# A fused attention and gated-MLP block: first pair of the last stage reordered, one store moved behind the last drain, another to a different queue

## The chip, the cores and the metric

The kernel runs on one core of one Trainium2 chip. The core has four computing engines that each work through a queue of their own in order: TensorE (PE), VectorE (DVE), ScalarE (ACT) and GpSimd (POOL). SyncE (SP) only issues transfers, and POOL issues some too. Sixteen DMA engines move the bytes. The metric is the device time of one execution in microseconds, as a median over several.

## The reference

All of it works on a normalised input `xn` of 2048 rows by 512 columns, in fp32:

```
xn  = layernorm(x)
q, k, v = split(xn @ wqkv)                    # 32 heads of 16
phi(t) = [softmax(t @ w_phi), softmax(-t @ w_phi)]    # per head, 32 features
kv  = phi(k)^T v ;  z = sum over rows of phi(k)
A   = (phi(q) kv) / (phi(q) z + 1e-6) @ wo
zz  = gelu(xn @ w_in) ;  z1, z2 = halves of zz (688 columns each)
g   = w_sp @ layernorm(z2) + b_sp             # w_sp: 2048 x 2048
B   = (z1 * g) @ w_out
out = x + A + B
```

## The kernel before

The 2048 rows are 16 tiles of 128. fp32 products are built from three matmuls: each operand is split into a rounded part and the rest (`round_h` on ACT, `rest_l` on DVE), and `mm3` (lines 52 to 55) multiplies high by high, high by low and low by high.

There are three stages. The first projects q, k, v and the MLP's first half, and writes the exponentials of q to HBM (`e_d`). The second multiplies `w_sp` by the normalised `z2`, with a seven-product scheme for 2 x 2 blocks, in eight rounds of two row tiles; `products` issues the matmuls, `drain` adds the seven PSUM tiles up, `gate` multiplies by z1, transposes the result on DVE (L732) and gives back a function that stores it block by block to HBM (`u_d`, four DMAs of 128-byte runs). The seventh round's gate (i = 6, `NP - 2`) is called inside the loop; the eighth round's drain stands behind the loop, and its gate is called late in the third stage, after the pair of tiles 8 and 9.

The third stage, which the change touches, handles the 16 query tiles in pairs. For a pair it

- finishes the features of each tile (`q_fin`, L487 to L494, eight DVE operations on a tile `et` loaded from `e_d`; tiles 0 and 1 come ready made as `eq`). From tile 4 on POOL copies the finished tile to a tile `er` by DMA (L842);
- transposes them on PE (`attend_T`: `ptq`, copied to `f` by ACT);
- multiplies by the key-value matrix `kvT` (`attend`: `po`, split into `oT` by ACT and DVE);
- multiplies the gated rows `u` (loaded by SP as `u` and `rt`, split into `uh` and `ul` by `gated`) by w_out into a PSUM tile `pout` (`project_u`);
- adds `oT` times wo to the same `pout` (`project_o`), adds the tile of x (`xr`, loaded by SP) on DVE (L913), and SP stores the sum to `out`.

There are two `pout` banks, so `project_u` of the next pair needs the xr addition of this one. `wof` are the raw rows of wo on their way to `wo_h` and `wo_l`.

The order on each engine is not written out: a scheduler places the instructions by its own estimate of when each is ready, in the order of the program text otherwise, and `tc.issue_after(x)` keeps what is inside it from being placed before x. Tiles of a pool that has been closed give their memory to later tiles, and a later tile waits for the last user of each byte it takes. A wait stands in the queue of the engine that issues, so everything behind it in that queue waits too. In the program before, the first pair is written out ahead of the loop (`project_u` 0, transposes, `project_u` 1, attention product), and the other pairs are in the loop.

Of the kernel before, what the change touches and what calls it, by code (L numbers as in the profile page):

```python
# [18 lines left out]
P = 128  # L19
# [18 lines left out]
def mixer(ctx: ExitStack, tc: tile.TileContext, x, x_t, wv, wqkT, phi_bd, wo, w_in, wst, b_r, w_out, out):  # L38
# [4 lines left out]
    def round_h(eng, h, src):  # L43
        if eng is act:
            return act.activation(h, src, AF.Copy).ins  # L45
        return eng.tensor_copy(h, src).ins

    def rest_l(l, src, h, eng=None):
        return (eng or dve).tensor_tensor(l, src, h.bitcast(F32), op=ALU.subtract).ins  # L49
# [429 lines left out]
    def load_q(s, et):  # L479
        sp.dma_start(et[:, :NF + 2 * H], e_d[s])  # L480
        return et

    def q_fin(et, tmp, zb):

        e, r, t, w = et[:, :NF], *(et[:, NF + k * 2 * H:NF + (k + 1) * 2 * H] for k in range(3))
        den = et[:, NF + 6 * H:QW]
        dve.tensor_tensor(tmp, e, zb, op=ALU.mult)  # L487
        dve.tensor_reduce(t, heads(tmp), axis=AX.X, op=ALU.add)
# [5 lines left out]
        return e, dve.tensor_tensor(heads(e), heads(e), bc(w, 2 * H), op=ALU.mult).ins  # L494
# [227 lines left out]
    def gate(i, cb, z, u, ut, after=None):  # L722
        cb, first, _ = cb
        with tc.issue_after(after or first):
            act.activation(z[:, :, :FH], z[:, :, :FH], AF.Gelu_apprx_tanh)
        zs = z[:, :, :FH].rearrange("p k (j f) -> p k j f", j=2)
        us = u[:, :, :FH].rearrange("p k (j f) -> p k j f", j=2)
        dve.tensor_tensor(us, zs, cb, op=ALU.mult)
        lo, hi = u[:, :, KF * P:FH], u[:, :, FH:FU].bitcast(F32R)
        dve.tensor_copy(hi, lo)  # L730
        rest_l(lo, lo, hi)
        dve.transpose(ut.rearrange("p k f -> p (k f)"), u.rearrange("p k f -> p (k f)"))  # L732

        def store():
            src = ut.rearrange("p k f -> p (k f)")
            dst = u_d[2 * i:2 * i + 2].rearrange("k (j a) t -> a (k j) t", a=BL)
            for b in range(0, P, BL):
                (sp if i < NP - 2 else pool).dma_start(dst[:, :, b:b + BL], src[b:b + BL].rearrange("p (m b) -> p m b", b=BL))

        return store  # L740

    def slot(name, dt=F32):
        return xz.tile([P, 2, FH], dt, tag="xz", name=name).rearrange("p a b -> p (a b)")
# [27 lines left out]
    lasts, wu = [None] * 7, []  # L771

    def first_q(s):
        e = slot("eq", F32R)[:, :NF]
        sp.dma_start(e.bitcast(F32), e_d[s, :, :NF])
        return e
# [12 lines left out]
    for n in range(NC):  # L789
        i = SEQ[n][0]  # L790
        if n % NQ == 1 and i < NP - 1:
            z = load_z1(i)
        products(n, g)
        if n % NQ == NQ - 1 and i < NP - 1:
            c = gt.tile([P, 2, FU], F32, tag="c", name="c")
            cq = c[:, :, :FH].rearrange("p k (j f) -> p k j f", j=2)
            cb = drain(i, g, cq)
            g = {}
        if n + 3 < NC:
            raw[n + 3] = load_a(n + 3)  # L800
        if n + 2 < NC:
            A[n + 2] = prep_a(n + 2, raw.pop(n + 2))
        if n % NQ == NQ - 1 and i < NP - 1:
            gate(i, cb, z, c, z, prep_a.last)()
        if n == NC - 4:
            stage_w()
        if n == NC - 3:
            zs = slot("zb", F32R)
            zb, ident_r = zs[:, :NF].bitcast(F32), zs[:, NF:NF + P]
            round_h(act, ident_r, ident)  # L810
            sp.dma_start(zb, zb_d)
            uT = [first_gate(0)]
            es[0], es[1] = first_q(0), first_q(1)
        if n == NC - 2:
            t = slot("u1", F32R)
            us = {1: load_u(1, k_tiles(t[:, :KF * P]).bitcast(F32), t[:2 * REM, KF * P:(KF + 1) * P])}
            ets[2], ets[3] = (load_q(s, slot("et")) for s in (2, 3))
    cb = drain(NP - 1, g, slot("c").rearrange("p (k j f) -> p k j f", k=2, j=2))
    with tc.issue_after(cb[1]), tc.issue_after(cb[2]):
        es[2], last = q_fin(ets.pop(2), slot("qtmp")[:, :NF], zb)  # L820
    mid.close()


# [32 lines left out]
    def attend_T(s):  # L856

# [15 lines left out]
    def attend(fs):  # L873

        oT = [wk.tile([P, NG, 2 * P], F32R, tag=f"oT{k}", name="oT") for k in "hl"]
        po = [pso.tile([P, 2, 2 * P], F32, tag="po", bufs=2, name="po") for _ in range(2)]
        for m in range(H // 2):
            k, c, r = m // 8, m // 2 % 4, m % 2  # L880
            rows, cols = slice(r * HP, (r + 1) * HP), slice(r * QP, (r + 1) * QP)
            lasts[3] = pe.matmul(po[r][c * QP:(c + 1) * QP, k], kvT[rows, m // 2, cols], fs[m // 4][rows, m // 2 % 2],
                                 start=True, stop=True).ins
        for r in range(2):
            qs = slice(r, None, 2)
            round_h(act, oT[0][:, qs], po[r])
            ins = rest_l(oT[1][:, qs], po[r], oT[0][:, qs])
        return oT, ins
# [26 lines left out]

    GATE_LAST = 8

    wo_h, wo_l = (cw.tile([P, ND, D], F32R, name=f"wo{k}") for k in "hl")
# [12 lines left out]
    def ahead(i):  # L931

        if 3 < i + 3 < NT:
# [2 lines left out]
            ets[i + 4] = load_q(i + 4, slot("et"))  # L936
            us[i + 4] = fetch_u(i + 4)

    nxt = {}
    for i in range(0, NT, 2):  # L940
        if i:
            p[i] = project_u(i, nxt.pop(i))
            if i + 2 < NT:
                nxt[i + 2] = gated(us.pop(i + 2))
            with tc.issue_after(lasts[2]):
                oT, _ = attend(fT)
            with tc.issue_after(lasts[3]):
                p[i + 1] = project_u(i + 1, nxt.pop(i + 1))
        else:
            nxt[2] = gated(us.pop(2))  # L950
        if i + 3 < NT:
            nxt[i + 3] = gated(us.pop(i + 3))
        for k in range(2):
            project_o(i + k, oT, p.pop(i + k))
            ahead(i + k)
        if i == 2:
            with tc.issue_after(lasts[6]):
                z = load_z1(NP - 1)
        if i == GATE_LAST:
            with tc.issue_after(lasts[0]), tc.issue_after(lasts[1]):  # L960
                gate(NP - 1, cb, z, z, gt.tile([P, 2, FU], F32, tag="zt", name="zt"))()
            p2.close()
        if i + 2 < NT:
            with tc.issue_after(lasts[4]):
                fT = attend_T(i + 2)
# [33 lines left out]
```

## Time and profile before

| | |
|---|---|
| median of 3 runs | 634.07 us (632.37 to 634.67) |
| the profiled execution | 633.23 us |
| its span | 631.5 us |
| granted TensorE clock | 1.00 |
| PE busy in the span | 621.9 us (98%) |
| DVE busy in the span | 517.8 us (82%) |
| last matmul of the second stage to the end | 495.2 to 631.5 us |

Times in a timeline are microseconds from the start of the span. A row of a timeline gives start, duration, engine, source line, operation and tiles; in brackets stands how long the engine was idle before it and what ended that. A duration is that of one instruction, and DVE and PE overlap the end of one with the start of the next, so the spacing of starts is what a chain of them costs. A row of a DMA view gives the issues, the size and the time from issue to landing. Line numbers are those of the kernel before; from line 732 on those of the changed kernel are 2 to 6 higher.

### The profile page before, as it was taken

What the parts mean: (1) busy time and instruction counts of PE and PEld (TensorE: products, weight loads), DVE (VectorE), ACT (ScalarE), POOL (GpSimd) and SP (SyncE); (2) the same over time, 40 slices, a digit from 0 to 9 for tenths busy, and PEclk for the clock granted to TensorE, in tenths of its full rate; (3) what the DMA queues carried; (4) which work ended last, traced back from release to release, by engine and by line L of the source; (5) the groups of instructions that cost most, each with busy time, mean ns of one, the idle gap of its engine ahead of it and who ended that gap; (6) DMA issues with size and microseconds to landing.
All of it is one profiled execution on the core that took longest, in us unless ns stands there. A gap on an engine that the chain in (4) does not pass through costs nothing.

```text
span 631.5 us, 11445 instructions
## 1 busy us (share of the span) xinstructions
PE 621.9 (98%) x4406; PEld 564.9 (89%) x4406; DVE 517.8 (82%) x908; ACT 270.9 (43%) x431; POOL 93.7 (15%) x176
## 2 busy tenths in 40 slices
PE   8999999999999999999999999999999989999997
PEld 6888888888888999999999999999999868877776
DVE  5999998987987768889989688696978789989622
ACT  5643434443333638877444343253444322223220
POOL 4142121111011015332000000000002001101100
PEclk9999999999999999999999999999999999999999
DMA  8455465354336941002463745637467798886930
GB/s 315 163 102 143 114 162 152 87 139 134 106 94 170 300 170 67 1 2 68 146 132 119 180 90 157 145 100 176 89 189 244 234 286 286 302 294 203 217 119 33
DMA packets 83574, 98.40 MB, mean 156 GB/s; under 512 B 40672, under 2 KB 53728, under 8 KB 83520
## 3 DMA queue, kind: packets, MB, share of 16 engines
q1 hardware_dynamic: 73088, 61.30, 33.1%
q0 software_dynamic: 8128, 30.74, 17.6%
q10 hardware_dynamic: 2304, 5.64, 2.3%
q8 instruction: 34, 0.56, 0.4%
q14 instruction: 20, 0.16, 0.1%
HBM read 56.37 MB, written 26.61 MB: 131 GB/s over the span
## 4 chain that ended last, share of the span: by engine, by line
PE 93%; DMA 2%; DVE 2%; SPq 1%; issue 0%; ACT 0%; POOL 0%; DVEq 0%; ACTq 0%; POOLq 0%
PE g L55 11%; PE g L54 11%; PE g L53 11%; PE proj L55 7%; PE proj L53 7%; PE proj L54 7%; PE zps L55 6%; PE zps L53 6%; PE zps L54 6%; PE pout L53 4%; PE pout L55 4%; PE pout L54 4%; DMA er<-et 2%; PE ptq L867 1%; PE kvps L312 1%; SPq L748 1%
## 5 line engine op out<-in xcount | busy, mean ns | idle before, releaser
L54 PE MATMUL g<-B,A 128*128 128x344 f32 x448 | 143.2, 320 | 0.0
L53 PE MATMUL g<-B,A 128*128 128x344 f32 x448 | 143.1, 319 | 0.0
L55 PE MATMUL g<-B,A 128*128 128x344 f32 x448 | 142.9, 320 | 0.0
L53 PEld LDWEIGHTS g<-B,A 128*128 128x128 f32 x448 | 84.2, 188 | 0.0
L55 PEld LDWEIGHTS g<-B,A 128*128 128x128 f32 x448 | 84.1, 188 | 0.0
L54 PEld LDWEIGHTS g<-B,A 128*128 128x128 f32 x448 | 84.1, 188 | 0.0
L45 ACT ACTIVATE A<-S 128x512 fp32r<-128x512 f32 x64 | 39.3, 628 | 77.5 <-DVE S L532 56.0
L113 ACT ACTIVATE e<-e,r_x 128x1024 f32<-128x1024 f32 x28 | 32.2, 1150 | 47.1 <-DVE e L112 46.6
L53 PE MATMUL proj<-wqk_h,xT 128*128 128x512 f32 x128 | 50.9, 398 | 0.0
L55 PE MATMUL proj<-wqk_h,xT 128*128 128x512 f32 x128 | 50.6, 395 | 0.0
L54 PE MATMUL proj<-wqk_l,xT 128*128 128x512 f32 x128 | 50.3, 393 | 0.0
L49 DVE TENSOR_TENSOR A<-S,A 128x512 fp32r<-128x512 f32 x64 | 43.3, 687 | 6.8 <-ACT A L45 6.6
L45 ACT ACTIVATE A<-wf 128x512 fp32r<-128x512 f32 x64 | 33.3, 521 | 31.7 <-PE g L55 14.9
L53 PE MATMUL zps<-w_0h,xT 128*128 128x344 f32 x128 | 41.4, 323 | 0.0
L55 PE MATMUL zps<-w_0h,xT 128*128 128x344 f32 x128 | 41.1, 321 | 0.0
L53 PE MATMUL zps<-w_1h,xT 128*128 128x344 f32 x128 | 41.0, 320 | 0.0
L55 PE MATMUL zps<-w_1h,xT 128*128 128x344 f32 x128 | 40.9, 320 | 0.0
L54 PE MATMUL zps<-w_0l,xT 128*128 128x344 f32 x128 | 40.9, 319 | 0.0
L54 PE MATMUL zps<-w_1l,xT 128*128 128x344 f32 x128 | 40.9, 319 | 0.0
L116 DVE TENSOR_REDUCE sm<-e 128x64 f32<-128x1024 f32 x28 | 33.9, 1209 | 5.8 <-ACT e L113 5.8
L49 DVE TENSOR_TENSOR A<-wf,A 128x512 fp32r<-128x512 f32 x64 | 35.2, 550 | 2.5 <-ACT A L45 2.3
L869 ACT ACTIVATE f<-ptq 128x512 f32<-128x512 f32 x32 | 16.5, 603 | 47.7 <-PE ptq L867 41.2
(208 smaller groups left out, 1410.1 us busy)
## 6 DMA issues: line engine op xcount, KB each, us to landing
wf<-in_wst SPq DMA_DIRECT2D x64, 256.0 KB, 3.4
e_d<-e POOLq DMA_DIRECT2D x16, 544.0 KB, 5.2
et<-e_d SPq DMA_DIRECT2D x16, 544.0 KB, 6.5
zacc<-e POOLq DMA_DIRECT2D x12, 512.0 KB, 4.6
er<-et POOLq DMA_DIRECT2D x12, 512.0 KB, 6.1
z_d<-z1f ACTq DMA_DIRECT2D x16, 344.0 KB, 3.1
z1t<-z_d POOLq DMA_DIRECT2D x16, 344.0 KB, 5.0
u<-u_d SPq DMA_DIRECT2D x15, 320.0 KB, 5.6
```

What stands on the lines that cost most here:

```text
L45: return act.activation(h, src, AF.Copy).ins
L49: return (eng or dve).tensor_tensor(l, src, h.bitcast(F32), op=ALU.subtract).ins
L53: pe.matmul(dst, ah, bh, start=start, stop=False)
L54: pe.matmul(dst, ah, bl, start=False, stop=False)
L55: return pe.matmul(dst, al, bh, start=False, stop=stop).ins
L113: act.activation(e, e, AF.Exp, scale=scale)
L116: dve.tensor_reduce(sm, heads(e), axis=AX.X, op=ALU.add)
L312: i = pe.matmul(kv_acc[k:k + QP, m // 4], vs[:, m * QP:(m + 1) * QP], e[:, m * HP:(m + 1) * HP], start=first and m < 4 and len(ready) == n ...
L748: sp.dma_start(t[rows:rows + r1 - r0], src[r0:r1, :])
L867: pe.transpose(pt[:, a, k].bitcast(F32R), src, ident_r)
L869: lasts[5] = act.activation(f, pt.rearrange("p a k b -> p a (k b)"), AF.Copy).ins
```

## The change

It has five parts.

1. `gate` no longer transposes; the function that it gives back does, and then stores. For the seventh round that function is called behind the last drain (in `issue_after(cb[2])`), not in the loop. Its four stores stay on POOL; those of the eighth round go from POOL to SP.
2. The third query tile (2) is loaded and finished two rounds earlier, ahead of the last drain; tiles 0 and 1 are loaded one round later than before.
3. The first pair goes into the loop: transposes first, then `project_u(0)`, the attention product, `project_u(1)`, `project_o`.
4. Some tiles are allocated earlier, and three placeholders (`xr`, `gap`, `oTh`) fix which memory the tiles of the last stage take. `er`, `wo`, `kvT`, `wof` and `u` then take memory that the seventh store does not read.
5. The PSUM pool of the transposes is opened before that of the products.

```diff
@@ gate
-        dve.transpose(ut.rearrange("p k f -> p (k f)"), u.rearrange("p k f -> p (k f)"))
-
-        def store():
+        def turn():
             src = ut.rearrange("p k f -> p (k f)")
+            dve.transpose(src, u.rearrange("p k f -> p (k f)"))
...
-                (sp if i < NP - 2 else pool).dma_start(...)
+                (pool if i == NP - 2 else sp).dma_start(...)
@@ second stage
-            gate(i, cb, z, c, z, prep_a.last)()
+            turn = gate(i, cb, z, c, z, prep_a.last)
+            if i < NP - 2:
+                turn()
...
             uT = [first_gate(0)]
+            ets[2] = load_q(2, slot("et"))
+            es[2], last = q_fin(ets.pop(2), slot("qtmp")[:, :NF], zb)
+        if n == NC - 2:
             es[0], es[1] = first_q(0), first_q(1)
-        if n == NC - 2:
...
-    with tc.issue_after(cb[1]), tc.issue_after(cb[2]):
-        es[2], last = q_fin(ets.pop(2), slot("qtmp")[:, :NF], zb)
+    with tc.issue_after(cb[2]):
+        turn()
@@ third stage
+    cw.tile([P, NF], F32R, tag="er", bufs=6, name="er")
+    wo_h, wo_l = (cw.tile([P, ND, D], F32R, name=f"wo{k}") for k in "hl")
...
+    pst = ctx.enter_context(psum("pst", 4))
     pso = ctx.enter_context(psum("pso", 1))
-    pst = ctx.enter_context(psum("pst", 4))
...
-    p = {0: project_u(0, uT.pop(0))}
     fT = attend_T(0)
+    wk.tile([P, D], F32, tag="xr", bufs=3, name="xr")
+    wk.tile([P, 40], F32, tag="gap", name="gap")
+    wk.tile([P, NG, 2 * P], F32R, tag="oTh", name="oT")
...
-    p[1] = project_u(1, uT.pop(0))
-    oT, ins = attend(fT)
-    fin.append(ins)
-    features(3)
...
     for i in range(0, NT, 2):
+        p[i] = project_u(i, nxt.pop(i))
+        if 0 < i < NT - 2:
+            nxt[i + 2] = gated(us.pop(i + 2))
+        with tc.issue_after(lasts[2]):
+            oT = attend(fT)
+        with tc.issue_after(lasts[3]):
+            p[i + 1] = project_u(i + 1, nxt.pop(i + 1))
+        if not i:
+            fin.append(lasts[7])
+            features(3)
```

On SP, behind the loads of wo, the queue before held the loads of query tiles 2 to 5, with the first xr (5703) among them and the features of tile 4 (5719) at its end:

```order
L753 DMA u_5637<-u_d_65 128x5x128
L754 DMA rt_5638<-u_d_65 96x128
L753 DMA u_5641<-u_d_65 128x5x128
L754 DMA rt_5642<-u_d_65 96x128
L902 DMA xr_5703<-in_x 128x512
L753 DMA u_5721<-u_d_65 128x5x128
L754 DMA rt_5722<-u_d_65 96x128
L902 DMA xr_5725<-in_x 128x512
L753 DMA u_5753<-u_d_65 128x5x128
L754 DMA rt_5754<-u_d_65 96x128
L902 DMA xr_5853<-in_x 128x512
L480 DMA et_5719<-e_d_63 128x1088
```

Now, from the third u on (the first xr is 5707, the features of tile 4 are 5723):

```order
L753 DMA u_5725<-u_d_65 128x5x128
L754 DMA rt_5726<-u_d_65 96x128
L908 DMA xr_5707<-in_x 128x512
L908 DMA xr_5729<-in_x 128x512
L753 DMA u_5757<-u_d_65 128x5x128
L754 DMA rt_5758<-u_d_65 96x128
L908 DMA xr_5857<-in_x 128x512
L754 DMA rt_5886<-u_d_65 96x128
L754 DMA rt_5918<-u_d_65 96x128
L480 DMA et_5723<-e_d_63 128x1088
```

The number of entries from the first xr to that et is the same, seven. What is new is what the first xr waits for: in the built program its tile lies on the source of the seventh store, and its entry waits for the transpose and for all four of POOL's blocks; before, it waited for an old DVE operation.

On DVE, between the first xr addition and the next pair's oT (po is the attention product of tiles 2 and 3), stood:

```order
L913 TENSOR_TENSOR xr_5703<-pout_5563,xr_5703 128x512
L913 TENSOR_TENSOR xr_5725<-pout_5645,xr_5725 128x512
L488 TENSOR_REDUCE et_5719<-qtmp_5741 128x64
L489 TENSOR_TENSOR et_5719<-et_5719 128x64
L490 SCALAR_TENSOR_TENSOR et_5719<-et_5719 128x32
L491 RECIPROCAL et_5719<-et_5719 128x32
L492 TENSOR_TENSOR et_5719<-et_5719 128x64
L494 TENSOR_TENSOR et_5719<-et_5719 128x1024
L487 TENSOR_TENSOR qtmp_5869<-et_5751,zb_5412 128x1024
L49 TENSOR_TENSOR ul_5804<-u_5721,uh_5803 128x640
L488 TENSOR_REDUCE et_5751<-qtmp_5869 128x64
L49 TENSOR_TENSOR oT_5808<-po_5809,oT_5807 128x2x256
```

Now the features of tile 4 begin (L487) ahead of that addition as they did before, and the two additions have L488 between them:

```order
L487 TENSOR_TENSOR qtmp_5745<-et_5723,zb_5407 128x1024
L919 TENSOR_TENSOR xr_5707<-pout_5631,xr_5707 128x512
L488 TENSOR_REDUCE et_5723<-qtmp_5745 128x64
L919 TENSOR_TENSOR xr_5729<-pout_5673,xr_5729 128x512
L489 TENSOR_TENSOR et_5723<-et_5723 128x64
```

The rest of tile 4's features, then L487 and L488 of tile 5 and a ul follow as before; behind that ul come the rest of tile 5's features and the start of tile 6's (5883) before oT:

```order
L49 TENSOR_TENSOR ul_5808<-u_5725,uh_5807 128x640
L489 TENSOR_TENSOR et_5755<-et_5755 128x64
L490 SCALAR_TENSOR_TENSOR et_5755<-et_5755 128x32
L491 RECIPROCAL et_5755<-et_5755 128x32
L492 TENSOR_TENSOR et_5755<-et_5755 128x64
L494 TENSOR_TENSOR et_5755<-et_5755 128x1024
L487 TENSOR_TENSOR qtmp_5905<-et_5883,zb_5407 128x1024
L49 TENSOR_TENSOR oT_5812<-po_5813,oT_5811 128x2x256
```

Between that ul and oT stood one operation before (L488 of tile 5), and six stand there now; L488 has moved ahead of the ul.

On POOL the stores of the eighth round (from `zt`) leave the queue that the er copies use:

```order
-L842 DMA er<-et 128x1024 x3
+L846 DMA er<-et 128x1024 x3
 L693 DMA z1t<-z_d 128x688 x2
-L842 DMA er<-et 128x1024 x6
-L738 DMA u_d<-zt 32x46x32 x4
-L842 DMA er<-et 128x1024 x3
-L995 UNCONDITIONAL_BRANCH
-L995 ISA
+L846 DMA er<-et 128x1024 x9
```

The nine copies behind the load of z1 now follow one another; the four stores stand on SP, behind the xr loads of tiles 10 to 12 and ahead of the u loads of tiles 14 and 15.

More of the change, by code (lines that the diff above doesn't have):

```diff
@@ L731, in gate @@
         rest_l(lo, lo, hi)
-        dve.transpose(ut.rearrange("p k f -> p (k f)"), u.rearrange("p k f -> p (k f)"))
-        def store():
+        def turn():
             src = ut.rearrange("p k f -> p (k f)")
+            dve.transpose(src, u.rearrange("p k f -> p (k f)"))
             dst = u_d[2 * i:2 * i + 2].rearrange("k (j a) t -> a (k j) t", a=BL)
             for b in range(0, P, BL):
-                (sp if i < NP - 2 else pool).dma_start(dst[:, :, b:b + BL], src[b:b + BL].rearrange("p (m b) -> p m b", b=BL))
-        return store
+                (pool if i == NP - 2 else sp).dma_start(dst[:, :, b:b + BL], src[b:b + BL].rearrange("p (m b) -> p m b", b=BL))
+        return turn
     def slot(name, dt=F32):
@@ L769, in first_gate @@
         return split_u(*u, k_tiles(a[:, n:2 * n]), k_tiles(b[:, :n]))
-    lasts, wu = [None] * 7, []
+    lasts, wu = [None] * 9, []
     def first_q(s):
@@ L812, in mixer @@
             uT = [first_gate(0)]
+            ets[2] = load_q(2, slot("et"))
+            es[2], last = q_fin(ets.pop(2), slot("qtmp")[:, :NF], zb)
+        if n == NC - 2:
             es[0], es[1] = first_q(0), first_q(1)
-        if n == NC - 2:
             t = slot("u1", F32R)
             us = {1: load_u(1, k_tiles(t[:, :KF * P]).bitcast(F32), t[:2 * REM, KF * P:(KF + 1) * P])}
-            ets[2], ets[3] = (load_q(s, slot("et")) for s in (2, 3))
+            ets[3] = load_q(3, slot("et"))
     cb = drain(NP - 1, g, slot("c").rearrange("p (k j f) -> p k j f", k=2, j=2))
-    with tc.issue_after(cb[1]), tc.issue_after(cb[2]):
-        es[2], last = q_fin(ets.pop(2), slot("qtmp")[:, :NF], zb)
+    with tc.issue_after(cb[2]):
+        turn()
     mid.close()
@@ L885, in attend @@
             qs = slice(r, None, 2)
-            round_h(act, oT[0][:, qs], po[r])
-            ins = rest_l(oT[1][:, qs], po[r], oT[0][:, qs])
-        return oT, ins
+            lasts[8] = round_h(act, oT[0][:, qs], po[r])
+            lasts[7] = rest_l(oT[1][:, qs], po[r], oT[0][:, qs])
+        return oT
     def project_u(i, u):
@@ L916, in mixer @@
     GATE_LAST = 8
-    wo_h, wo_l = (cw.tile([P, ND, D], F32R, name=f"wo{k}") for k in "hl")
-    p = {0: project_u(0, uT.pop(0))}
     fT = attend_T(0)
+    wk.tile([P, D], F32, tag="xr", bufs=3, name="xr")
+    wk.tile([P, 40], F32, tag="gap", name="gap")
+    wk.tile([P, NG, 2 * P], F32R, tag="oTh", name="oT")
     with tc.issue_after(lasts[5]), tc.issue_after(lasts[1]), tc.issue_after(fin[-1]):
@@ L937, in ahead @@
             us[i + 4] = fetch_u(i + 4)
-    nxt = {}
+    p, nxt = {}, dict(enumerate(uT))
     for i in range(0, NT, 2):
[L941 to L951, printed above, removed]
+        p[i] = project_u(i, nxt.pop(i))
[8 more added lines that the diff above has]
+            features(3)
+            with tc.issue_after(lasts[7]), tc.issue_after(lasts[8]):
+                nxt[2] = gated(us.pop(2))
+        if i < NT - 2:
             nxt[i + 3] = gated(us.pop(i + 3))
```

## The prediction

> **What bounds the kernel now.** I read the totals first, then the waits of PE, then the chain of work that ended last, then the timelines of PE, DVE, POOL and SP around the last stage.
>
> ```profile
> PE 621.9 (98%) x4406; PEld 564.9 (89%) x4406; DVE 517.8 (82%) x908; ACT 270.9 (43%) x431; POOL 93.7 (15%) x176
> ...
> PE pout L53 <- ACT oT L45: 2.1, 1, 2.1
> PE ptq L867 <- DMA er<-et: 1.4, 1, 1.4
> PE pout L53 <- DVE xr L913: 0.2, 1, 0.2
> ...
> 585.22 10.60 DMA er<-et
> ```
>
> TensorE works 621.9 of 631.5 us. The change removes no matmul, so it can win only pauses of PE in the last stage, which the three rows of PE's waits show: 2.1 + 1.4 + 0.2 = 3.7 us, 0.6% of the time (the last row is the chain's, behind the 1.4). Anything it makes PE wait for is a loss. Below, u(i) and o(i) are the products with w_out and wo for query tile i, f(i) the eight DVE operations that finish the features of tile i (L487 to L494), and T the moment at which the seventh store's last block has landed.
>
> **The first pair's new order.** PE's timeline of the first pair, then from the chain the second pair:
>
> ```profile
> 495.24 0.40 PE L53 MATMUL pout<-wu,u_uh 128*128 128x512 f32 x1
> ...
> 507.78 0.50 PE L53 MATMUL pout<-woh,oT 128*128 128x512 f32 x1 [2.08 <-ACT oT L45]
> ...
> 515.87 0.50 PE L53 MATMUL pout<-wu,uh 128*128 128x512 f32 x1 [0.20 <-DVE xr L913]
> ...
> 521.10 0.43 PE pout L53
> 525.22 0.23 PE pout L53
> 530.68 1.32 PE ptq L867 x16
> 531.99 0.30 PE pout L53
> ```
>
> Before, the attention product ends the pair's preparation and o(0) has to wait 2.08 us for oT. Now the transposes come first and u(1) stands between the attention product and o(0). u(1) lasts 4.1 us (521.10 to 525.22 for its like), which covers the rounding of oT on ACT and DVE. That pause and the 0.20 before u(2) would go: with nothing else in the way u(2) starts at 515.87 - 2.08 - 0.20 = 513.6.
>
> **The third query tile, earlier.** f(2) leaves the place after the last drain and goes before it, and the transpose of the seventh block goes from 478 to behind the last drain.
>
> ```profile
> 478.12 1.71 DVE L732 STREAM_TRANSPOSE z1t<-c 128x1472 f32<-128x1472 f32 x1
> 490.77 0.58 DVE L711 SCALAR_TENSOR_TENSOR c<-g,bias,c 128x344 f32<-128x344 f32 x1 [3.19 <-PE g L55]
> 494.08 1.06 DVE L711 SCALAR_TENSOR_TENSOR c<-g,bias,c 128x344 f32<-128x344 f32 x2
> 495.44 0.58 DVE L711 SCALAR_TENSOR_TENSOR c<-g,bias,c 128x344 f32<-128x344 f32 x1 [0.31 <-PE g L55]
> ...
> L775 SPq DMA_DIRECT2D eq<-e_d x2: 424/748/1073, 481.8 to 482.3; - x2
> eq<-e_d SPq DMA_DIRECT2D x1, 512.0 KB, 6.4
> ...
> 497.07 0.82 DVE L49 TENSOR_TENSOR ul<-u,uh 128x640 fp32r<-128x640 f32 x1
> 508.01 1.28 DVE L49 TENSOR_TENSOR oT<-po,oT 128x512 fp32r<-128x512 f32 x2
> 509.21 1.22 DVE L487 TENSOR_TENSOR qtmp<-et,zb 128x1024 f32<-128x1024 f32 x1
> 510.46 1.22 DVE L488 TENSOR_REDUCE et<-qtmp 128x64 f32<-128x1024 f32 x1
> ...
> 512.85 1.23 DVE L494 TENSOR_TENSOR et<-et 128x1024 f32<-128x1024 f32 x1
> 513.99 1.22 DVE L487 TENSOR_TENSOR qtmp<-et,zb 128x1024 f32<-128x1024 f32 x1
> 515.13 1.28 DVE L913 TENSOR_TENSOR xr<-pout,xr 128x512 f32<-128x512 f32 x2
> ```
>
> f takes 513.99 - 509.21 = 4.8 us. DVE's 3.19 us pause before 490.77 and the 1.71 us of the transpose make room for 4.9. The tile's load takes the queue place of the eq load above, issued at 481.8 and landed 6.4 us later at 488.2. f(2) then ends at 493.0 at the latest, the first drain comes up to 2.2 us late, and the drains catch up to within 0.5 us, because they had waited for PE between one another. PE's second transpose tile needs the bank that the 494.08 pair frees, 0.4 us before PE is there. I take 0 and keep 0 to 0.5 us. The bank order of the two PSUM pools costs nothing for the same reason.
>
> **The seventh store, later.** This is the term that decides. The transpose now starts at 496.0 (the end of the 495.44 row) and lasts 1.7. POOL's issue followed its transpose by 0.6 us at 480.45 and by about 1 us at 581.34, so the store begins at about 498.5. How long it takes to land, from three like stores (the timeline's rows, then first and last start of four issues, and the landing of the last), and two stretches of the windows view, whose last three columns are granted clock, share of the DMA engines and GB/s:
>
> ```profile
> 452.94 3.98 SPq L738 DMA_DIRECT2D u_d<-z1t  x4
> 460.58 1.07 POOL L693 DMA_DIRECT2D z1t<-z_d  x2 [24.54 <-DMA u_d<-z1t]
> ...
> L738 POOL DMA_DIRECT2D u_d<-z1t x4: 902/908/947, 480.4 to 483.2; - x4
> u_d<-z1t POOLq DMA_DIRECT2D x1, 184.0 KB, 9.0
> L738 POOL DMA_DIRECT2D u_d<-zt x4: 902/915/934, 581.3 to 584.3; - x4
> u_d<-zt POOLq DMA_DIRECT2D x1, 184.0 KB, 10.2
> ...
> 498.00:502.00 4.00, 4.00 (x29) 3.46 (x28) 3.24 (x6) 2.32 (x5) 0.00 (x0) 1.00 0.48 145
> 506.00:510.00 4.00, 2.22 (x10) 1.72 (x10) 2.83 (x5) 1.71 (x3) 0.00 (x0) 1.00 1.09 328
> ```
>
> Nearly alone: 460.6 - 452.9 = 7.6 us. Among other loads: 483.2 + 9.0 - 480.4 = 11.8 and 584.3 + 10.2 - 581.3 = 13.2. Here half of the DMA engines' time is taken at first (0.48) and all of it (1.09) once the loads of u run, so I take 10.5, between the two: T = 509.0, bounds 506.1 and 511.7.
>
> Who waits for T: the first xr tile lies on the store's source, so its load on SP waits for all four blocks, and every later entry of SP's queue with it. The queue before:
>
> ```profile
> 493.05 7.97 SPq L748 DMA_DIRECT2D wof<-in_wo  x16
> 501.06 0.42 SPq L753 DMA_DIRECT2D u<-u_d  x1
> 503.19 0.37 SPq L902 DMA_DIRECT2D xr<-in_x  x1
> 506.86 0.38 SPq L480 DMA_DIRECT2D et<-e_d  x1
> et<-e_d SPq DMA_DIRECT2D x1, 544.0 KB, 5.9
> DMA to landing us min/median/max: 3.5/6.2/10.6
> ...
> 594.54 0.37 SPq L753 DMA_DIRECT2D u<-u_d  x1
> ```
>
> That SP stands still for a store is seen at 594.54, the moment at which the eighth store landed (594.5). Before, xr was issued at 503.19, and the et load of tile 4, seven issues later, 3.7 us behind it; it landed 5.9 after that, 9.6 from the xr. In the new order seven issues again lie between. From T to that landing it is therefore at least 3.7 + 3.5 (the shortest et landing; the last fenced row but one) = 7.2, at most 9.6. I take 8.0, nearer to the short end, since the loads ahead of xr have drained by T. So et(4) lands at 517.0. It matters because DVE runs strictly in its written order: L487 of f(4) stands ahead of the add that empties o(0)'s bank, and u(2) needs that bank. 517.0 + 1.14 (513.99 to 515.13) + 0.65 (half of the xr pair and its handover) = 518.8: u(2) starts 2.9 us later than before instead of 2.3 earlier.
>
> **The second pair.** From there DVE's new order counts. Between the first xr add and oT it now holds L488 to L492 of f(4) with the other xr add among them, L494, the whole of f(5), one ul and L487 of f(6). By the spacing of the rows above: 2.4 (510.46 to 512.85) + 0.6 + 1.15 + 4.8 + 0.7 + 1.1 = 10.75, and 0.6 for the first oT: 11.35 after the start of u(2). PE comes to the fifth matmul of o(2), the first that needs it, after 525.22 - 515.87 + 4 x 0.23 = 10.3: 1.1 us of waiting. The next xr add stands at the end of the rest of f(6), a ul and L487 of f(7): 18.0 after the start of u(2), where PE before needed 531.99 - 515.87 = 16.1. Together the pair costs 1.85 us more. From the following pair on DVE comes clear: two f, two ul, two oT and two xr are 9.6 + 1.5 + 1.3 + 1.3 = 13.7 us in a pair of 16.1.
>
> **The eighth store, on SP.** Before, POOL issues it ahead of the er copy of tile 13, which starts at 585.22 and lands 10.6 later, so PE waits 1.4 at 594.5. Now POOL's queue holds only copies and tile 13's features stand ahead of the gate on DVE: minus 1.4. On SP the four issues cost 4.0 us (the 452.94 row) ahead of the loads of tiles 14 and 15, which at 594.54 were still in time; nothing added.
>
> **Sum.** u(2) +2.9, second pair +1.85, er -1.4: +3.35 us. The profiled execution took 633.23 (span 631.5 and 1.7 around it), 0.84 under the median of 634.07. It comes to 636.6 against that execution and 637.4 against the median.
>
> **A slower clock after the wait** (a rival to this sum). PE would stand from 513.6 to 518.8, 5.2 us. The longest pause before is 2.08, and the clock stays at 1.00 across it (the stretch from 506, above). If a pause this long halves the clock for all of u(2), its 4.1 us double; 1.85 of the added 4.1 lie where PE waits for DVE anyway, so the sum rises by 2.25: 639.7. [...]
>
> **Rivals.**
> - The store lands early and the change is not slower. The point that decides: u(2) may start as late as 515.4 (515.87 + 1.4 - 1.85) before the sum turns positive, so et(4) by 513.6 and T by about 505.6 to 506. For it speaks the store that took 7.6 us (T = 506.1); against it, that the u loads share the engines here. If T no longer binds at all: -2.3 + 1.85 - 1.4 = -1.85, 632.2.
> - All pauses go and DVE keeps up: 634.07 - 3.7 = 630.4, faster by 0.6%. It needs an early T and a second pair without the 1.1 us wait for oT; the sum of DVE's rows speaks against it.
> - The store lands as slowly as at 581 (T = 511.7) and et after 9.6: u(2) at 523.1, +7.2 + 1.85 - 1.4 = +7.7, 641.8.
>
> **How the numbers follow.** Half a percent, about what a measurement of this kernel can tell from no change, is 3.2 us: 630.9 and 637.2. The likeliest, a blocked SP queue, gives 635 to 640 (chance 0.58); the early store 631.5 to 635 (0.22); everything won 630.4 (0.08); the slow store or the slow clock 640 to 643 (0.12). Slower: somewhat over half of the first case and all of the last, 0.5; faster 0.1; the same 0.4. The range drops the fully won case and the far end: 632.5 to 641.
>
> **What the new profile would show.** Right: no wait of o(0) for oT; SP idle before the first xr load until the seventh store lands near 509; PE idle before u(2), released by the DVE add, behind a DVE wait for et; about 1 us of PE waiting for oT in the second pair; no PE wait for er near 594. Wrong: an xr load before 505, u(2) starting before 515, or a clock below 1.00 after the wait. The prediction fails most likely through T, which I took from stores that ran beside other traffic.

## The result: 639.6 us, 1.0% slower

The changed kernel takes 639.61 us (median of 4 runs, 638.91 to 640.70) against 633.75 us for the kernel before on the same chip: a ratio of 1.0096, 95% interval 1.0070 to 1.0122. The forecast was 637.4 us with 632.5 to 641.0; by its own sum +3.35 us, measured +5.9.

The profiled execution took 640.23 us with a span of 638.5. Its second stage ends at 496.04 us, 0.8 later than before; the whole trace stands 0.8 later, and in the profiles of the experiments this end varies between 495.3 and 496.0 with no relation to what was edited. I take the 0.8 off wherever the two traces are compared.

The changed kernel's view of waits for PE (us in total, times, longest):

```profile
PE pout L53 <- DVE xr L919: 4.1, 3, 2.6
PE pout L53 <- ACT oT L45: 2.6, 1, 2.6
...
PE pout L55 <- DVE oT L49: 0.8, 1, 0.8
```

And from PE's timeline the first matmuls of o(0), u(2) and u(10), with the wait in brackets:

```profile
509.38 0.79 PE L53 MATMUL pout<-woh,oT 128*128 128x512 f32 x1 [2.57 <-ACT oT L45]
...
520.99 0.47 PE L53 MATMUL pout<-wu,uh 128*128 128x512 f32 x1 [2.64 <-DVE xr L919]
...
588.25 0.51 PE L53 MATMUL pout<-wu,uh 128*128 128x512 f32 x1 [1.29 <-DVE xr L919]
```

The wait of o(0) for oT is still there, 2.57 us instead of 2.08, although u(1) now stands in front of it. u(2) starts 520.99 - 0.8 - 515.87 = 4.3 us later than before. The er wait (1.4) has gone and one of 1.29 at u(10) has come. The queues behind the first two waits, from the timelines of SP, ACT and DVE of the changed kernel:

```profile
490.12 13.75 SPq L748 DMA_DIRECT2D wof<-in_wo  x16
...
508.58 0.52 SPq L754 DMA_DIRECT2D rt<-u_d  x1
509.40 0.83 SPq L908 DMA_DIRECT2D xr<-in_x  x2
...
512.88 0.36 SPq L480 DMA_DIRECT2D et<-e_d  x1
...
508.21 0.63 ACT L45 ACTIVATE woh<-wof 128x512 fp32r<-128x512 f32 x1 [5.47 <-DMA wof<-in_wo]
508.74 1.07 ACT L45 ACTIVATE oT<-po 128x512 fp32r<-128x512 f32 x2
...
519.02 1.23 DVE L487 TENSOR_TENSOR qtmp<-et,zb 128x1024 f32<-128x1024 f32 x1 [2.25 <-DMA et<-e_d]
520.16 0.69 DVE L919 TENSOR_TENSOR xr<-pout,xr 128x512 f32<-128x512 f32 x1
```

From the chain of work that ended last, the wo load that ACT's row at 508.21 waits for; from SP's view of waits the one that the sixteen wo entries hold; and the landing times of the store's four blocks, issued from 499.1 to 501.8:

```profile
502.10 6.08 DMA wof<-in_wo
...
SPq L748 <- PE ptq L873: 4.0, 1, 4.0
...
DMA to landing us min/median/max: 4.6/5.9/6.8
```

Three things can be read here. A wo load issued at 502.10 needs 6.08 us where the median before was 2.0, and ACT rounds oT behind the fourth wo block, so o(0) waits for a weight load. The store's last block, issued at 501.8, landed 6.8 us later, at 508.6. And SP comes to the first xr only at 509.1, when its rt issue of 508.58 is over. So xr did not wait for the store whose source it overwrites; the 0.3 us up to its issue at 509.40 are not that wait. The forecast had SP standing in front of that store; SP was late before it got there. Part of SP's delay is not slow loads: 4.0 of the 13.75 us are one wo entry's wait for PE's transposes, behind which the other entries stand.

The windows view of the changed kernel shows what went on meanwhile (last three columns: granted clock, share of the DMA engines, GB/s). The DMA engines are full and move half of what they move at 506 to 510 us before (1.09 and 328):

```profile
500.00:504.00 4.00, 4.00 (x46) 2.65 (x45) 1.39 (x2) 0.66 (x2) 2.71 (x4) 1.00 0.95 163
504.00:508.00 4.00, 2.81 (x13) 1.92 (x11) 0.00 (x0) 0.00 (x0) 0.00 (x0) 1.00 0.92 178
```

### The profile page after: what moved, and what is told of

It reads as the page before. It is cut to its first block, busy times and chain, and to the rows that moved or that the text cites. A ratio compares the mean times of both kernels' runs of the same rounds, so it can differ in the third digit from the quotient of the medians.

```text
span 638.5 us, 11434 instructions
## 1 busy us (share of the span) xinstructions
PE 625.4 (98%) x4406; PEld 566.8 (89%) x4406; DVE 517.4 (81%) x908; ACT 270.3 (42%) x431; POOL 89.0 (14%) x172
## 4 chain that ended last, share of the span: by engine, by line
PE 89%; DMA 4%; DVE 4%; SPq 1%; issue 1%; ACT 0%; DVEq 0%; POOLq 0%
PE g L55 11%; PE g L54 11%; PE g L53 11%; PE proj L55 7%; PE proj L53 7%; PE proj L54 7%; PE zps L55 6%; PE zps L53 6%; PE zps L54 6%; PE pout L53 4%; PE pout L54 3%; PE pout L55 3%; PE kvps L312 1%; PE pt L268 1%; DMA u<-u_d 1%; DMA wof<-in_wo 1%
```

## The experiments

Twelve kernels ran, in three groups: the first four told here, then the square together with q2_late, then the rest. With each group the kernel before ran on the same chip (634.64, 634.39 and 634.53 us). Ratios are to it, with 95% intervals. A trace is that of one execution, which can lie some us from its median.

**xr off the store's source.** The er tiles change places with xr in the memory, both in their first use and as placeholders:

```diff
-    cw.tile([P, NF], F32R, tag="er", bufs=6, name="er")
...
+    wk.tile([P, NF], F32R, tag="er", bufs=6, name="er")
```

> The changed kernel with the xr tiles moved off the seventh store's source (they change places with the tiles of er, which are first written much later), so that no entry of SP's queue waits for that store. Theory A, the prediction's (SP's queue stands behind the xr load until the store has landed): xr is issued about when SP is free, et(4) lands some 4 us earlier, u(2) starts near 516 instead of 521.0 (as the trace has it), and the time falls by 3 to 4 us, to 635.5 to 636.5. Theory B (the store's many small packets take the DMA engines, so that the loads of wo and u ahead of xr are late by themselves): SP reaches the xr load at about 509 as before, u(2) stays within 0.5 us of 521.0, o(0) still waits some 2.5 us for oT, and the time stays at 639 to 640.

Measured 640.24 us, ratio 1.0084 (1.0053 to 1.0114). Its timelines of SP and PE:

```profile
509.74 0.52 SPq L754 DMA_DIRECT2D rt<-u_d  x1
510.30 0.90 SPq L907 DMA_DIRECT2D xr<-in_x  x2
...
509.86 0.79 PE L53 MATMUL pout<-woh,oT 128*128 128x512 f32 x1 [3.47 <-ACT oT L45]
```

xr follows the rt load without a gap, and nothing is won: theory A falls. The edit is not quite clean, since kvT moved too and its load, and with it the wo loads, began 5 us later (at 495.3). That alone does not decide it: in the changed kernel itself the store had landed before SP came to xr. The trace is of an execution of 644.31 us, 4.1 above the median, with the three stretches of half clock that the last section shows.

**The seventh store early again.** The block's transpose and store go back into the loop, all else stays:

```diff
-            if i < NP - 2:
-                turn()
+            turn()
...
-    with tc.issue_after(cb[2]):
-        turn()
```

> The changed kernel with the seventh block's transpose and store back at their old place, behind the gate of that block (near 480 us), everything else as changed. Theory B: with no store between 499 and 509 us the wo blocks land in about 2 us each instead of 6, o(0) no longer waits for oT, u(2) starts at 513.6 to 516, and the time is 632 to 635: what is left over the time before is DVE's new order in the second pair. Theory A gives the same time, but has o(0) still waiting 2.5 us, since it puts nothing on the store's traffic. Rival C (the loss comes from the new order of the first pair or from DVE's order, and not from the store): u(2) stays later than 518 and the time above 637.

Measured 630.88 us, ratio 0.9948 (0.9929 to 0.9967): faster than the kernel before. Its waits of PE have none of o(0) for oT; the longest in the last stage is 1.6 us, for an er copy. From its timelines of PE and SP the start of u(2) and the issue of et(4):

```profile
514.43 0.47 PE L53 MATMUL pout<-wu,uh 128*128 128x512 f32 x1 [0.74 <-ACT f L872]
...
505.37 0.38 SPq L480 DMA_DIRECT2D et<-e_d  x1
```

So the late store alone costs 1.5% (1.0096 against 0.9948), some 9 us, and the rest of the change gains 3 to 4. But this edit changed more than the store. With the store early, the scheduler also gives other orders: five entries stand between the wo loads and et(4) on SP instead of thirteen (it is issued at 505.37 instead of 512.88), and ACT and DVE round oT ahead of the fourth wo block. (The expectation of order_early below has four and eleven entries, which is too few.) Traffic and order are mixed in it; the square below takes them apart.

**The store held back.** The transpose stays behind the last drain, the four issues are written behind o(1), xr as in the first experiment:

```diff
+        if i == 0:
+            with tc.issue_after(lasts[4]):
+                store7()
```

> The changed kernel with xr off the store's source as in the run xr_clear, the transpose of the seventh block left behind the last drain, but the four issues of its store held back until the last matmul of o(1), near 530 us, where no weight load is under way. Theory B: the wo blocks land in about 2 us, o(0) does not wait for oT, u(2) starts at 514 to 517 and the time is 633 to 636, as far below the run xr_clear as the run store_early is. Theory A: nothing is won over the run xr_clear. Something may be given back later, since er copies stand behind the store in POOL's queue: a wait of PE of up to 2 us behind 535 us would show that.

Measured 640.22 us, ratio 1.0092 (1.0067 to 1.0116). It did not do what it was for. `issue_after` orders only what is on the engine of the instruction named, here PE; POOL had nothing in front of the store and issued it as soon as the transpose, which ends at 497.84, was over (the row names ACT's copies, which end 0.1 us later):

```profile
498.46 3.63 POOL L741 DMA_DIRECT2D u_d<-z1t  x4 [35.78 <-ACT f L877]
```

The orders on all engines are those of the first experiment, so this is a second measurement of it, and says nothing on a later store.

**The eighth store back on POOL.**

```diff
-                (pool if i == NP - 2 else sp).dma_start(...)
+                (sp if i < NP - 2 else pool).dma_start(...)
```

> The changed kernel with the eighth store back on POOL, everything else as changed. The prediction's term (the er copy of tile 13 stands behind the store in POOL's queue and PE waits 1.4 us for it): the wait near 594 us comes back and the time rises by 1.4 us, to 641. Rival (the gain is not real: with the store on SP the wait of 1.3 us for the add of xr at 587 us has taken its place): the wait at 587 us goes or shrinks, and the time stays within 0.5 us of 639.6.

Measured 640.01 us, ratio 1.0085 (1.0059 to 1.0111): no difference from the changed kernel. Neither the er wait nor the one at u(10) appears in its profile. SP's timeline has a gap of 1.2 us ahead of xr, with the same order up to there. Here the store landed later, at 509.4, and SP's view of waits puts 0.9 us down to it. So theory A's wait exists in this run, but it is no more than the gap:

```profile
507.78 0.56 SPq L754 DMA_DIRECT2D rt<-u_d  x1
509.51 0.83 SPq L908 DMA_DIRECT2D xr<-in_x  x2
```

**The square: traffic and order apart.** Theory T was now that the store's traffic delays the loads; theory O that the scheduler, which has the late transpose and store in its own estimate, gives an order that waits. Orders can be exchanged: a table at the end of the program chains the instructions of DVE, ACT, SP and PE in the order that the other kernel has, without any wait for completion.

```diff
+ORDER = {"DVE": (...), "ACT": (...), "SP": (...), "PE": (...)}
+def follow(tc, nc):
+    traced = {i.name: i for i in nc.cur_bb.bb.instructions}
+    for numbers in ORDER.values():
+        for a, b in zip(numbers, numbers[1:]):
+            tc.add_manual_dep(traced[f"I-{b}"], f"I-{a}", NoSync, reason="order")
```

Store late, order of the early store:

> The run xr_clear (store late, xr off its source) with the orders of DVE, ACT, SP and PE written out as the planner gives them when the store is early; the transpose and the four issues of the store stay behind the last drain. In that order oT is rounded before the fourth wo block, the load of et(4) stands four issues behind the wo loads instead of eleven, and both adds of the first pair stand together on DVE. Theory T (the store's traffic delays the loads of wo, u and et, whatever the order): still 637 to 640, o(0) still waits for oT by 2 us or more. Theory O (the planner, which sees the late transpose and store in its own time line, gives another order, and that order waits): 631 to 634, with o(0) waiting under 1 us and u(2) at 514 to 517.

Store early, order of the late store:

> The opposite corner: transpose and store of the seventh block early, as in the run clear_early, but the orders of DVE, ACT, SP and PE written out as the planner gives them when the store is late. Theory T: with the traffic gone from 499 to 509 us the time is 631 to 633. Theory O: 636 to 640, with u(2) at 518 or later behind et(4). If the two multiply (a late issue is only costly where loads are slow), both corners lie near 633 to 636.

Both early, with xr off the store's source (the first two edits together):

> The run store_early with the xr tiles off the place of the seventh store's source; the planner gives the same orders as in store_early. It is the corner of the square that the runs order_early and order_late are read against. Both theories: within 0.5% of the run store_early, 630 to 632.5, faster than before by about 0.5%.

| | order of the early store | order of the late store |
|---|---|---|
| store early | clear_early 632.31 us, 0.9972 (0.9953 to 0.9990) | order_late 636.18, 1.0031 (1.0016 to 1.0046) |
| store late | order_early 636.87, 1.0033 (1.0008 to 1.0058) | xr_clear 640.24, 1.0084 (1.0053 to 1.0114) |

The order alone costs 1.0031 - 0.9972 = 0.6%, 3.7 us, the late store alone as much (0.6%), and both together 1.1%: they add, within the intervals. (xr_clear is of the first group, on another chip; clear_early stands 0.2% above store_early, with intervals that overlap.) Neither theory is right alone. How each acts is in the rows. First order_early (order early, store late), its waits of PE:

```profile
PE ptq L870 <- DVE et L494: 2.7, 1, 2.7
PE ptq L872 <- DMA er<-et: 2.6, 1, 2.6
...
PE pout L53 <- ACT oT L45: 1.5, 1, 1.5
```

And in its timelines the third wo block on ACT and et(4) on SP:

```profile
506.23 0.63 ACT L45 ACTIVATE woh<-wof 128x512 fp32r<-128x512 f32 x1 [5.05 <-DMA wof<-in_wo]
...
509.58 0.38 SPq L480 DMA_DIRECT2D et<-e_d  x1
```

The wo loads are late, oT behind the third of them too, and DVE runs late into the features of tile 3. SP needs 11.6 us for its sixteen wo issues, where clear_early, with the same order, needs 7.4; in neither does one of them wait for another engine. (The wait of 2.6 for an er copy is 1.4 in clear_early; this execution took 640.12 us, 3.2 above the median.) Then order_late (store early), timelines of SP, DVE and PE:

```profile
510.15 0.37 SPq L480 DMA_DIRECT2D et<-e_d  x1
...
516.37 1.22 DVE L487 TENSOR_TENSOR qtmp<-et,zb 128x1024 f32<-128x1024 f32 x1 [3.19 <-DMA et<-e_d]
...
518.34 0.77 PE L53 MATMUL pout<-wu,uh 128*128 128x512 f32 x1 [3.57 <-DVE xr L915]
```

Here o(0) does not wait at all, although oT stands behind the fourth wo block. What costs is et(4) thirteen entries back on SP, and DVE's L487 ahead of the xr add, as the forecast had it. u(2) starts 518.34 - 514.30 = 4.0 us later than in clear_early. Behind this pause the clock is halved (0.50 granted from 518.5 to 524.0), and u(2) takes 6.8 us instead of 4.1: in this trace 2.7 of the 5.3 us between the two spans (635.8 and 630.5) are the slower clock.

**Is it the traffic, and is it its bytes?** With the transpose left early, the store is issued a second time at the late place, to the same area, or to a scratch area in rows of 5.9 KB; orders as in clear_early. Of the two stores below, the first stands in dup_late and the second in dup_wide, both behind the last drain and held there by the copy of two columns:

```diff
+            dve.tensor_copy(src[:, :2], src[:, :2])
+            for b in range(0, P, BL):
+                pool.dma_start(dst[:, :, b:b + BL], src[b:b + BL].rearrange(...))
+                pool.dma_start(w_d[b:b + BL], src[b:b + BL])
```

> The run clear_early, with its orders written out on every engine, and the seventh block stored a second time, from the same tile to the same place, behind the last drain: DVE only rewrites two columns there, to hold the second store back until then, and the 1.7 us transpose is not repeated. So the orders and DVE's work are those of the early store, and only the traffic of 499 to 509 us is added. Theory T (traffic alone makes the loss that the run order_early shows against clear_early, 4.5 us): 635.5 to 638, with o(0) waiting 1 to 1.5 us for oT behind the third wo block. Rival (the late transpose on DVE makes it): within 1 us of clear_early, 631 to 633.

> As the run dup_late, but the second store goes to a scratch area of its own in rows of 5.9 KB instead of runs of 128 bytes: the same 736 KB in four issues on POOL. Were the bytes what counts, the time would be as in dup_late, 635.5 to 638. If it is the number of small packets, the four issues land in 2 to 4 us, the third wo block is hardly late, and the time stays within 1 us of clear_early: 631 to 633.

dup_late: 636.12 us, ratio 1.0035 (1.0013 to 1.0057), as order_early without the late transpose on DVE. dup_wide: 633.81 us, 0.9989 (0.9972 to 1.0006). The timelines of dup_late at o(0) and at the third wo block:

```profile
507.80 0.50 PE L53 MATMUL pout<-woh,oT 128*128 128x512 f32 x1 [1.62 <-ACT oT L45]
506.64 0.63 ACT L45 ACTIVATE woh<-wof 128x512 fp32r<-128x512 f32 x1 [2.53 <-DMA wof<-in_wo]
```

That block in the timelines of clear_early and of dup_wide:

```profile
502.94 0.63 ACT L45 ACTIVATE woh<-wof 128x512 fp32r<-128x512 f32 x1 [1.51 <-DMA wof<-in_wo]
...
504.74 0.63 ACT L45 ACTIVATE woh<-wof 128x512 fp32r<-128x512 f32 x1 [0.18 <-DMA wof<-in_wo]
```

The windows view of clear_early, with neither store, from 500 to 504 us:

```profile
500.00:504.00 4.00, 4.00 (x45) 2.67 (x44) 1.72 (x3) 1.69 (x4) 0.00 (x0) 1.00 0.57 143
```

The same of dup_late:

```profile
500.00:504.00 4.00, 4.00 (x46) 2.65 (x45) 0.64 (x1) 0.53 (x1) 1.08 (x2) 1.00 0.96 173
```

And of dup_wide:

```profile
500.00:504.00 4.00, 4.00 (x46) 2.65 (x45) 0.69 (x1) 0.51 (x2) 0.00 (x0) 1.00 0.82 245
```

The traffic alone makes the loss of order_early; the transpose on DVE has no part in it that can be measured. The third block comes to ACT 3.7 us later than in clear_early with the short runs and 1.8 with the long rows, which is soon enough for o(0) not to wait for oT. The same bytes in long rows cost 0.2% instead of 0.6%, and that interval includes no cost. The engines are then 0.82 busy at 245 GB/s instead of 0.96 at 173, so it is mainly the runs of 128 bytes.

**The other parts alone.** From store_early, the third query tile's features go back behind the last drain (the lines of the kernel before); from that, the eighth store back on POOL; and the kernel before with only the eighth store on SP.

> The run store_early with the third query tile's features back behind the last drain: against the kernel before, only the first pair's order and the queue of the eighth store then differ. The prediction has the earlier features at no cost and the second pair at +1.85 us through DVE's order, of which the place of f(2) is one part: by its terms this run has 634.1 - 2.3 for the first pair, and er 0 to -1.4: 630.4 to 632. Rival (f(2) behind the last drain is what held oT and so o(0) in the first pair): o(0) waits for oT again by 1 us or more, and the time is 633 to 635.

> The run q2_late with the eighth store back on POOL: against the kernel before, only the first pair is ordered as in the changed kernel. The prediction's terms: minus 2.3 us for the first pair, the er wait of 1.4 us stays: 631.9 to 632.3 where before is at 634.4. Rival (the eighth store's queue gives nothing, as the run eighth_pool says): as q2_late, 630.5, and no er wait near 594.

> The kernel before with nothing changed but the queue of the eighth store, SP instead of POOL; the orders of all other engines are the same. The prediction's term: the er wait of 1.4 us near 594 goes, 633.0 where before is at 634.4, 0.2% faster. Rival: SP's four issues hold the loads of the last tiles back or the wait only changes its name: within 0.5 us of before, and the trace has a wait of like length near 594.

q2_late: 630.50 us, 0.9950 (0.9934 to 0.9967). pair_only: 632.10 us, 0.9956 (0.9932 to 0.9980). eighth_only: 632.67 us, 0.9980 (0.9964 to 0.9997). The places that decide, first in PE's timeline of pair_only:

```profile
513.60 0.47 PE L53 MATMUL pout<-wu,uh 128*128 128x512 f32 x1 [0.26 <-ACT f L872]
597.54 2.05 PE L870 MATMUL ptq<-zb,er 128*128 128x128 f32 x15 [2.25 <-DMA er<-et]
```

And in that of eighth_only:

```profile
509.06 0.77 PE L53 MATMUL pout<-woh,oT 128*128 128x512 f32 x1 [2.79 <-ACT oT L45]
```

pair_only keeps the memory places and the PSUM order of the change, so it is parts 3 to 5 of it. It gains 2.4 us between the medians: u(2) starts at 513.6, and the er wait stays (2.25 in this execution, whose span of 634.6 lies above the median). Both together, q2_late, are not measurably better than pair_only, so the two gains do not simply add. The eighth store alone gains 0.2%, 1.3 us by the ratio and 1.9 between the medians: the er wait is gone and only the old wait of o(0) is left. The earlier features change nothing (q2_late and store_early agree within 0.1%). The best versions are q2_late and store_early, 0.5% faster than the kernel before and 1.5% faster than the changed one.

## Why the forecast was right in its sign and wrong in its mechanism

The wait on which the forecast rests, SP's for the store, did not occur in the profiled execution. That its largest term, u(2) +2.9, still comes near the measured 4.3 is luck: SP came late to xr for another reason, at 509.1 (508.3 with the 0.8 off), close to the 509.0 that the forecast had for the end of the store.

- **First pair, -2.3 us: right as a pause, and not cashed in.** pair_only starts u(2) at 513.6, the very figure of the forecast, and gains 2.4 us by the medians. That the gain agrees too is a coincidence of two things that the forecast did not have: the slower products with wo (below) cost pair_only about 1 us, and it runs more often at full clock (6 of 11 executions at 1.00, the kernel before 6 of 32 in that group). The means of these executions are 631.9 and 633.3, only 1.4 apart. In the changed kernel o(0) still waits. The step "with nothing else in the way" failed: I counted the store's transfer against the xr load and never against the wo loads, which run in the same 10 us and stand ahead of oT on ACT.
- **Third query tile earlier, 0: right** (store_early against q2_late).
- **Seventh store: right in its sign, wrong in its cause, and too small.** The step was "the first xr tile lies on the store's source, so its load on SP waits". T itself was well placed: the last block landed at 508.6, 507.8 with the 0.8 taken off, where 509.0 was forecast, with bounds of 506.1 and 511.7. But SP came to xr after that, at 509.1, because of the slow loads ahead of it and one wo entry's wait for the transposes; clearing xr from the source wins nothing. What costs is the traffic of small packets (0.6%) and the order that the scheduler gives because of the late store (0.6%). I priced the late store at 2.9 + 2.3 = 5.2 us; taken out, it gives 1.5%, about 9, of which the square accounts for 1.1%.
- **From xr to et(4), 8.0 us: mis-sized.** It took the long end, counted from xr's issue: 512.88 - 509.40 = 3.5 of issues and 519.0 - 512.9 = 6.1 for the landing, 9.6. I had taken the short end because "the loads ahead of xr have drained by T"; they had not: ACT waits until 511.06 for a u load that SP issued at 506.72, ahead of xr, and the engines are full (1.04) from 509 to 512, in the last section's windows. These 1.6 us more, with xr issued 0.4 earlier than forecast (508.6 against 509.0), make most of the 1.4 by which u(2) was later than forecast (4.3 against 2.9).
- **Second pair, +1.85: +1.5.** From u(2) to u(4) 538.48 - 520.99 = 17.5 us against 531.83 - 515.87 = 16.0; the wait of o(2) for oT is 0.8 (forecast 1.1).
- **Eighth store, -1.4: right alone, not here.** eighth_only confirms it. In the changed kernel the er wait went too, but u(10) waits 1.29 for an xr add whose chain begins with L487 of the next features waiting 2.25 for its et load, and going back to POOL (eighth_pool) changes nothing that can be measured. POOL's timeline in eighth_pool shows why the er wait does not come back:

```profile
581.49 0.53 POOL L846 DMA_DIRECT2D er<-et  x1 [5.92 <-DVE et L494]
589.80 0.93 POOL L738 DMA_DIRECT2D u_d<-zt  x1 [7.78 <-DVE et L492]
```

The copy of tile 13 goes out at 581.49, ahead of the store; before, it stood behind the store (585.22). The forecast named both reasons, the queue and the new place of tile 13's features on DVE; the second alone is enough here. The wait at u(10) does not come from the queue alone: xr_clear has one of 2.14 there and store_late, with the same orders, has none.
- **Slower clock: a rival that came true in part and did not decide the profiled execution.** The forecast tied it to a pause of 5.2 us at u(2). Here it came with the 2.57 us pause at o(0) instead, and its cost (the transposes behind o(1) start at 516.42, 7.0 us after o(0) instead of 5.6) was hidden, since u(2) waited for DVE until 520.99 anyway. In order_late it was not hidden (above). No run shows the term behind the 639.7, a half clock for all of u(2) after a pause of 5.2 us: the half clock in the changed kernel lasted 3.41 us, and in order_late, behind 3.57 us, u(2) took 6.8 us instead of 4.1.
- **Missing from the sum:** the products with wo run 0.15 us slower per pair (below), about 1 us over the kernel.

With these the span comes out: u(2) +4.3, second pair +1.5, and from u(4) to the end +0.4 (er -1.6 and u(10) +1.5 by the starts of the products, five slower pairs +0.75, the last tile -0.3): +6.2, as 638.5 - 631.5 - 0.8.

## What to carry to other kernels

A moved store is not only late for those who wait for it: here its packets, in runs of 128 bytes, slowed the loads that ran beside it (a wo load took 6.08 us, where the median was 2.0), with the engines full and half the bandwidth (0.95 at 163 GB/s, against 1.09 at 328). Look up which loads share its time, and which engine queues stand behind those loads. Where a scheduler places instructions by its own estimates, moving one transfer reorders others; compare the orders, and exchange them by a table, before a difference in time is put down to the transfer.

## What the runs showed that I had not expected

**Behind a pause of 2.57 us the clock was 0.50, behind one of 2.64 it was 1.00.** The changed kernel around both pauses, windows view (the first number behind the length is PE's busy time, the third from the end the granted clock):

```profile
505.50:509.00 3.50, 1.31 (x6) 0.74 (x4) 0.13 (x1) 0.79 (x2) 0.00 (x0) 0.99 0.85 194
508.50:509.00 0.50, 0.00 (x0) 0.00 (x0) 0.13 (x1) 0.50 (x2) 0.00 (x0) 0.96 0.76 207
509.00:512.00 3.00, 2.62 (x6) 2.14 (x7) 3.00 (x5) 2.17 (x4) 0.00 (x0) 0.50 1.04 293
512.00:512.50 0.50, 0.50 (x3) 0.37 (x3) 0.50 (x1) 0.00 (x0) 0.00 (x0) 0.63 0.91 262
517.50:520.90 3.40, 0.85 (x8) 0.61 (x6) 1.88 (x3) 1.97 (x4) 0.00 (x0) 1.00 1.03 309
521.00:524.00 3.00, 3.00 (x13) 2.47 (x14) 2.86 (x7) 0.00 (x0) 0.00 (x0) 1.00 0.46 172
```

Taken as mixes of the 1.00 and 0.50 of the rows around them, 0.96 in the second row puts the fall at 508.96 and 0.63 in the fourth the return at 512.37: 3.41 us at half clock. The run xr_clear has three such stretches; these are the half microseconds in which they begin:

```profile
508.50:509.00 0.50, 0.00 (x0) 0.00 (x0) 0.50 (x1) 0.31 (x1) 0.00 (x0) 0.63 0.33 72
...
522.00:522.50 0.50, 0.50 (x2) 0.41 (x3) 0.50 (x1) 0.00 (x0) 0.00 (x0) 0.78 0.20 78
...
590.50:591.00 0.50, 0.00 (x0) 0.00 (x0) 0.50 (x3) 0.00 (x0) 0.00 (x0) 0.55 0.00 0
```

Read in the same way they begin at 508.63, 522.28 and 590.55: 13.65 and 68.27 us apart, 4 and 20 times 3.41. My estimate from these figures alone is that where a pause lies in such steps counts beside its length: of the 2.57 us (from 506.81) 2.15 lie in the 3.41 us ahead of the fall at 508.96, and the 2.64 us (518.35 to 520.99) lie with 0.84 and 1.80 on the two sides of 519.19 (508.96 + 3 x 3.41). The 3.41 us ahead of 508.96 held 1.3 us of matmuls. In other profiles the clock was 1.00 across 2.08 us (before, to 507.78); the slices of about 15.8 us that hold a pause of 2.25 us (pair_only, to 597.54) and one of 2.79 (eighth_only, to 509.06) have a granted clock between 0.8 and 0.9, and half clock came with the 3.47 us in xr_clear and the 3.57 in order_late. What decides it was not tried.

**The products with wo became slower by 2.6%.** PE's timeline before, the first of the 24 matmuls of a pair with wo and the transposes behind the last one:

```profile
540.99 0.40 PE L53 MATMUL pout<-woh,oT 128*128 128x512 f32 x1
...
546.45 1.47 PE L867 MATMUL ptq<-zb,er 128*128 128x128 f32 x16
```

The same pair after:

```profile
547.68 0.40 PE L53 MATMUL pout<-woh,oT 128*128 128x512 f32 x1
...
553.28 1.49 PE L873 MATMUL ptq<-zb,er 128*128 128x128 f32 x16
```

24 matmuls take 5.46 us before and 5.60 after, at full clock and without a pause, while the products with w_out take the same 4.1 us. All runs made from the changed kernel have 5.6, eighth_only, made from the kernel before, has 5.47. The memory places of wo and oT and the order in which the two PSUM pools are opened differ between the two groups; which of them does it was not tried. The forecast had the bank order at nothing; this leaves up to 1 us on it.
